# Attention, a dense MLP and a routed mixture in one Trainium2 kernel: table stores by row, and four kinds of loads in another order

## The chip, the cores and the metric

The kernel runs on one NeuronCore of one Trainium2 chip. The metric is device time of one execution in microseconds (us), the median of several runs. Below, PE is TensorE, DVE VectorE, ACT ScalarE, POOL GpSimd, and SP the engine whose queue issues nearly all DMA transfers.

## What is computed

Three layers, each feeding the next, all in float32: attention of 4 batches, 8 heads, 576 positions, head size 64, with a local mask (4 heads) or a strided mask (4 heads); a dense MLP over 2304 tokens of width 512 with 2048 hidden units; and a mixture of 8 experts in which every token goes to one.

```python
# attention: scores under mask_local (0 <= rel < 32) or mask_strided (same position modulo 32)
attn = softmax(where(mask, q @ k.T / 8, -1e9));  a = attn @ v
# dense
h = maximum(a @ w_in, 0);  x = (s * h * h + b) @ w_out
# routed: the expert of a token is the largest logit of its own
e_idx = argmax(x @ w_gate);  p = softmax(x @ w_gate)[e_idx];  eom = sigmoid(x @ w_output_gate)
out[mask_e] = p * eom[:, e] * (maximum(x @ w1[e], 0) @ w2[e])
```

## The kernel before

The tokens stand in five units of 256, 512, 512, 512 and 512. Stage one goes over 30 attention groups (scores `L586`, transposes of the probabilities `L657`, values `L696`) and, in between, over the dense products of each unit (`L915`, `L919`, `L953`), whose hidden weights come as 64-bit words (`raw`, `L774`) and are made into operands by DVE. The first nine groups share their buffers with those weights. Stage two first finds, per token, the best expert and its scale (probability times gate, `scl`). One expert is predicted for all tokens, and its two products are computed for every unit in steps of about 10 us by a scheme that saves products (seven instead of eight blocks): PE `L1480` forms the blocks, DVE adds them up in `su`, `dd` and `ht`, PE `L1426` is the second product. The operands come from `xd`, the copy of `x` in device memory: `load_x` loads them (`xr`, two transfers a unit, `L1275`), DVE forms four differences (`tt`, `L1299`) and rounds all to operands `x` (`L1185` on ACT, `L1189` on DVE). Tokens with another expert than the predicted one are listed by expert in tables (`index`: `gid`, `sid`, `lsd`), gathered (`extra`: their `x` as `X`, columns copied to `xe`, their scales fetched by an indirect DMA on POOL, `se`) and computed apart; `merge_rows` and the last tile put their rows into the output.

Two small tables pass through device memory. `scd` holds the scale of each token, so that the gather can fetch it by row number: `L1144` stores `scl` (128 partitions, one column per 128 tokens, 10 and then 8 columns) with each 4-byte element its own piece. `kid` holds the slot of every token; `keep` (`L1715` to `L1723`) stores its 18 columns likewise, 2304 pieces of 4 bytes, and later loads the last 128 back as `kix`, which `merge_rows` (`L1559`) reads.

The order of work is not written out by hand. Every piece is a generator that yields `op(...)` with an engine, an estimated duration, what it waits for, and a priority; a list scheduler picks the piece that can start first, with the priority added to its start (a lower one goes earlier). The instructions of each engine then stand in that order and each engine goes through its own strictly. All plain DMAs go through SP's queue in that order too: one that waits holds all behind it. `LOADS` and `FIRST_LOADS` set the order of the first transfers: `q` (queries with keys of a group), `v` (its values), `w` (a weight tile of 512 KB).

Of the kernel before, what the change touches and what calls it, by code (L numbers as in the profile page):

```python
# [6 lines left out]
F32 = mybir.dt.float32  # L7
F32R = mybir.dt.float32r
I32 = mybir.dt.int32
AF = mybir.ActivationFunctionType  # L10
ALU = mybir.AluOpType
# [52 lines left out]
P_DVE = 2.0  # L64
P_LATE = 0.7
P_X0 = 0.5
P_INDEX = 0.4
P_INDEX_PE = -0.3
P_EVAC = 1.5
# [93 lines left out]


WQ, WV = 1024, 768
LOADS = [(g, k) for k in range(2) for g in range(3)] + [(g, k) for g in range(3, len(GROUPS)) for k in range(2)]
FIRST_LOADS = "qqqvwvwvwqvwqvwqvwqvwqvwqvw"
LATE_Q = [k / 1000 for k, x in enumerate(FIRST_LOADS) if x in "qv"]
LATE_W = [k / 1000 for k, x in enumerate(FIRST_LOADS) if x == "w"]

# [127 lines left out]
def op(*engs, waits=(), dep=True, on=(), late=0.0):  # L298
    return engs, waits, dep, on, late
# [6 lines left out]
def body(ctx, tc, qkv, w12, moe_s, moe_b, wg, e12, out):  # L306
# [14 lines left out]
    ps = enter(tc.tile_pool(name="ps", bufs=2, space=PSUM))  # L321

    xd = [dram.tile([P, KD, USZ[u]], F32, name=f"xd{u}") for u in range(NU)]
    scd = dram.tile([NT, 1], F32, name="scd")
    gid = dram.tile([SLOT, NTAB + 1], I32, name="gid")
    sid = dram.tile([SLOT, NTAB + 1], I32, name="sid")
    lsd = dram.tile([SLOT, 2], I32, name="lsd")
    kid = dram.tile([NT, 1], I32, name="kid")

    MW = 2 * LK  # L330
    mk = const.tile([P, MW + 2 * P], F32R, name="mk")
# [24 lines left out]
    ones = const.tile([QT, P], F32, name="ones")  # L356
    poh = const.tile([P, E], F32, name="poh")
    pint = const.tile([P, 1], I32, name="pint")
    kix = const.tile([P, 1], I32, name="kix")
    xsl = mx.tile([P, 4 * sum(WIDE.values())], F32R, name="xsl", tag="big", bufs=1)  # L360
    xk = {"S": xsl[:, 0:4 * WIDE["S"]].rearrange("p (c h t) -> p c h t", c=2, h=2),
          "L": xsl[:, 4 * WIDE["S"]:].rearrange("p (c h t) -> p c h t", c=2, h=2)}
# [166 lines left out]
    def load_qkv(at):  # L529
        g, k = LOADS[at]  # L530
        w = widths(g)[k]
        yield op(("DMA", 0.0014 * w), waits=([t_qe if g < NEARLY else t_qv] if k == 0 else []) + ([t_w] if g < NEARLY else []),
                 late=LATE_Q[at] if at < len(LATE_Q) else P_QKL)
        if g < NEARLY:
            t = wp.tile([P, w], F32, name="qkv", tag="w")
        else:
            t = at_pool.tile([P, (WQ, WV)[k]], F32, name="qkv", tag=("qk", "vv")[k], bufs=NQV)[:, 0:w]
        wq = widths(g)[0]
        nc.sync.dma_start(out=t, in_=qkv[g, k * P * wq:P * (wq + k * w)].rearrange("(p n) -> p n", n=w))
        qkvs[g, k] = t  # L540
        o.set(ev_qkv[g, k], o.fin + DMA_LAT)
        if at + 1 < len(LOADS):
            o.spawn(load_qkv(at + 1), after=False)
# [224 lines left out]

    def load_w64(at):
        j = WSEQ[at]  # L770
        yield op(("DMA", 1.46), waits=[t_rw, t_w] + ([ev_early] if at >= NGATE else []), late=LATE_W[at] if at < len(LATE_W) else 0.0)
        t = wp.tile([P, 512, 2], I32, name="raw64", tag="w")
        fc, n = divmod(j, 2)
        nc.sync.dma_start(out=t, in_=w12[fc].bitcast(I32)[:, n * 1024:(n + 1) * 1024].rearrange("p (f t) -> p f t", t=2))  # L774
        raw64[j] = t
        o.set(ev_r[j], o.fin + DMA_LAT)
        if at == 12:
            o.spawn(consts())
        if at + 1 < 2 * NF:
            o.spawn(load_w64(at + 1), after=False)  # L780
# [325 lines left out]
    def route(t0, t1):  # L1106
        n = t1 - t0

        def bc(v):
            return v.unsqueeze(2).to_broadcast([QT, n, E])  # L1110

        lm, lo = lg[:, t0:t1, 0:E], lg[:, t0:t1, E:2 * E]
        yield op(("DVE", 0.7))
        m = rs(n)
        nc.vector.tensor_reduce(out=m, in_=lm, axis=AX.X, op=ALU.max)
        d = rt(n)
        nc.vector.tensor_sub(out=d, in0=lm, in1=bc(m))
        v = rt(n)
        nc.vector.scalar_tensor_tensor(out=v, in0=d, scalar=0.0,
                                       in1=wt[0:QT].unsqueeze(1).to_broadcast([QT, n, E]),  # L1120
                                       op0=ALU.is_equal, op1=ALU.mult)
        yield op(("DVE", 0.7))
        mv = rs(n)
        nc.vector.tensor_reduce(out=mv, in_=v, axis=AX.X, op=ALU.max)
        hot = oh[:, t0:t1, :]
        nc.vector.tensor_tensor(out=hot, in0=v, in1=bc(mv), op=ALU.is_equal)
        g = rt(n)
        nc.vector.tensor_mul(out=g, in0=lo, in1=hot)
        yield op(("DVE", 0.25))
        sg = rs(n)  # L1130
        nc.vector.tensor_reduce(out=sg, in_=g, axis=AX.X, op=ALU.add)
        yield op(("ACT", 0.4))
        ex = rt(n)
        nc.scalar.activation(out=ex, in_=d, func=AF.Exp)
        nc.scalar.activation(out=sg, in_=sg, func=AF.Exp, scale=-1.0)
        yield op(("DVE", 0.68))
        se = rs(n)
        nc.vector.tensor_reduce(out=se, in_=ex, axis=AX.X, op=ALU.add)
        nc.vector.tensor_scalar(out=se, in0=se, scalar1=1e-9, scalar2=None, op0=ALU.add)
        nc.vector.scalar_tensor_tensor(out=se, in0=sg, scalar=1.0, in1=se, op0=ALU.add, op1=ALU.mult)  # L1140
        nc.vector.reciprocal(out=scl[:, t0:t1], in_=se)
        yield op(("DMA", 1.0))
        with nc.allow_non_contiguous_dma(reason="one scale a token"):
            nc.sync.dma_start(out=scd[t0 * QT:t1 * QT, :].rearrange("(t p) o -> p (t o)", p=QT),  # L1144
                              in_=scl[:, t0:t1])

    ev_p = Ev()

# [118 lines left out]
    def load_x(s):  # L1267
# [11 lines left out]
        if s == 0:  # L1279
            for c, (t, ev) in enumerate(raws):  # L1280
                yield op(("SP", 0.0), waits=[ev, [t_xa]], dep=False)
                x, _ = x_tile([P, 2, 2, n])
                yield from parts(t, [x[:, h] for h in range(2)])
                x2[s, c] = x
                o.free(t_w)
            o.set(ev_x2[s, "X"])
            o.spawn(load_x(1), prio=0.1)
            return
        (r0, e0), (r1, e1) = raws
        src = {"B11": r0[:, :, 0:hn], "B21": r1[:, :, 0:hn], "B22": r1[:, :, hn:]}  # L1290
# [16 lines left out]
            o.free(t_w)  # L1307
            o.free(t_g)
        if s + 1 < NS:
            o.spawn(load_x(s + 1), prio=0.1)  # L1310

    acc2 = {}
    ev_scl = Ev()
# [238 lines left out]

    def merge_rows(oe, gc):

        yield op(("DVE", 1.6), waits=[ev_kid, ev_scl, t_w])
        t = wp.tile([P, 1024], F32, name="mr", tag="w")
        own, kf, tf, rows = t[:, 0:1], t[:, 1:2], t[0:SLOT, 2:4], t[:, 1024 - DM:]
        nc.vector.memset(rows, 0.0)
        nc.vector.tensor_copy(out=kf, in_=kix)  # L1559
        nc.vector.scalar_tensor_tensor(out=own, in0=kf, scalar=float(NT), in1=scl[:, NT // P - 1:], op0=ALU.is_lt, op1=ALU.mult)  # L1560
        nc.vector.tensor_copy(out=tf[:, 0:1], in_=gc[0:SLOT, 1:2])
        nc.vector.tensor_scalar(out=tf[:, 1:2], in0=tf[:, 0:1], scalar1=float(NT - P), scalar2=float(OOB), op0=ALU.is_lt, op1=ALU.mult)
        nc.vector.tensor_scalar(out=tf[:, 0:1], in0=tf[:, 0:1], scalar1=float(P - NT), scalar2=None, op0=ALU.add)
        place = mx.tile([SLOT, 1], I32, name="pl", tag="pl", bufs=1)
        nc.vector.tensor_tensor(out=place, in0=tf[:, 0:1], in1=tf[:, 1:2], op=ALU.add)
        yield op(("DMA", 1.0))
        nc.sync.dma_start(out=pd, in_=rows)
        yield op(("POOL", 1.1))
        nc.gpsimd.indirect_dma_start(out=pd, out_offset=bass.IndirectOffsetOnAxis(ap=place, axis=0),
                                     in_=oe, in_offset=None, bounds_check=P - 1, oob_is_err=False)  # L1570
        ev = Ev()
        o.set(ev, o.fin + 5.0)
        yield op(("DMA", 1.0), waits=[ev])
        nc.sync.dma_start(out=rows, in_=pd)
        o.fin += DMA_LAT
        merge.update(own=own, rows=rows)
        o.set(ev_merge)

    ev_kid, ev_half = Ev(), [Ev(), Ev()]


    ex = {}
# [2 lines left out]
    def index():  # L1585
# [55 lines left out]
        nc.vector.tensor_copy(out=ai, in_=adr)  # L1641
        nc.vector.tensor_single_scalar(out=si, in_=ai, scalar=SLOT - 1, op=ALU.bitwise_and)
        nc.vector.tensor_single_scalar(out=ci, in_=ai, scalar=SLOT.bit_length() - 1, op=ALU.logical_shift_right)
        o.spawn(keep(ki), prio=0.5)
        slf, clf = (tb[0:QT, k:k + NQT] for k in (816, 840))
        yield op(("DVE", 0.2))
        nc.vector.tensor_copy(out=slf, in_=si)
# [64 lines left out]
        ex["li"], ex["lrow"] = li, lrow  # L1712
        o.spawn(first_extra(), prio=P_EXTRA, pe=P_EXTRA_PE)

    def keep(ki):  # L1715
        yield op(("DMA", 1.0))
        with nc.allow_non_contiguous_dma(reason="one number a token"):
            nc.sync.dma_start(out=kid.rearrange("(t p) o -> p (t o)", p=QT), in_=ki)
        ev = Ev()
        o.set(ev, o.fin + 17.0)  # L1720
        yield op(("DMA", 0.1), waits=[ev])
        nc.sync.dma_start(out=kix, in_=kid[NT - P:, :])
        o.set(ev_kid, o.fin + 6.0)  # L1723

    def extra(get, n=NT):
        src = mx.tile([P, KD, NT], F32, name="X1", tag="big", bufs=1)
        for u in range(NU):
# [6 lines left out]
        with nc.allow_non_contiguous_dma(reason="one column of a table"):  # L1734
            nc.sync.dma_start(out=gr, in_=gid[:, bass.ds(c, 1)].rearrange("s o -> o s"))
            for h in range(2):
# [1 line left out]
            nc.sync.dma_start(out=gc[0:SLOT, 1:2], in_=sid[:, bass.ds(c, 1)])  # L1738
        t_gr = Ev()
        o.set(t_gr, o.fin + 3.0)  # L1740
        yield op(("POOL", 1.1), waits=[t_gr])
        se = mx.tile([P, 1], F32, name="se", tag="se", bufs=1)
        nc.gpsimd.indirect_dma_start(out=se, out_offset=None, in_=scd,
                                     in_offset=bass.IndirectOffsetOnAxis(ap=gc[:, 0:1], axis=0))
        yield op(("DVE", 1.8), waits=[t_r])
        xe = mx.tile([P, KD, SLOT], F32, name="xe", tag="r", bufs=NR)
        for k in range(0, SLOT, 4):
# [186 lines left out]
```

## Time and profile before

| | us |
|---|---|
| median of 3 runs | 708.28 (707.63 to 709.64) |
| the profiled execution | 711.24 |
| its span, first to last instruction | 709.5 |
| PE busy in it | 692.3 |
| mean granted TensorE clock | 0.987 |

Times in the rows are us from the start of the span. "Idle before" is time in which an engine stood before an instruction, with the one that ended it behind the arrow. An engine that waits costs time only if PE comes to wait for it in turn. The granted clock (PEclk) is a share of TensorE's full speed; 0.50 is 1.2 GHz, 1.00 is 2.4 GHz.

### The profile page before, as it was taken

The numbers are of one execution on the slowest core, as the hardware profiler recorded it, in microseconds if no ns is written. First come the engines' busy times: TensorE is split into PE (matmuls) and PEld (weight loads), VectorE is DVE, ScalarE is ACT, GpSimd is POOL, SyncE is SP. The second block draws the span as 40 slices with busy tenths as digits, with TensorE's granted clock in tenths as the row PEclk, the third lists the DMA queues.
The fourth block names the chain that finished last, engine by engine and source line by source line (L and its number), as shares of the span: only waits on it lengthen the run. The fifth ranks groups of instructions, "written<-read, shape, count | busy, mean of one in ns | idle before, by whom it ended". The sixth has DMA issues, their size and how long they took to land. (4 is left out here: it accounts for less than half of the span.)

```text
span 709.5 us, 11984 instructions
## 1 busy us (share of the span) xinstructions
PE 692.3 (98%) x4704; PEld 581.2 (82%) x4704; DVE 363.9 (51%) x853; ACT 301.0 (42%) x630; POOL 25.2 (4%) x100
## 2 busy tenths in 40 slices
PE   7999999999999999999999999999978999999996
PEld 6888888898777777877788878888977999898895
DVE  5798888854244342254341234444647754654440
ACT  4677554645344433344433544545321432323221
POOL 5000000022000000000000000001000000000000
PEclk9799999999999999999999999999998999999999
DMA  8974433241231112026200131111050073341201
GB/s 313 405 292 129 169 101 102 94 134 56 89 115 60 41 54 69 1 92 88 66 1 1 58 121 61 59 59 62 0 79 13 24 261 111 118 171 78 70 11 64
DMA packets 32622, 69.02 MB, mean 97 GB/s; under 512 B 8749, under 2 KB 11822, under 8 KB 31794
## 3 DMA queue, kind: packets, MB, share of 16 engines
q1 hardware_dynamic: 32434, 68.20, 29.5%
q8 instruction: 38, 0.62, 0.4%
q14 instruction: 22, 0.18, 0.1%
q0 software_dynamic: 128, 0.02, 0.0%
HBM read 56.75 MB, written 11.70 MB: 96 GB/s over the span
## 5 line engine op out<-in xcount | busy, mean ns | idle before, releaser
L919 PE MATMUL h<-xsl,w 128*128 128x512 f32 (+1 forms) x876 | 206.9, 381 | 0.0
L953 PE MATMUL bk<-g,w 128*128 128x512 f32 (+1 forms) x864 | 203.5, 381 | 0.0
L919 PEld LDWEIGHTS h<-xsl,w 128*128 128x128 f32 x876 | 155.7, 188 | 31.4 <-issue 0.8
L953 PEld LDWEIGHTS bk<-g,w 128*128 128x128 f32 x864 | 153.4, 188 | 31.7 <-issue 2.1
L867 ACT ACTIVATE r<-h 128x512 f32<-128x512 f32 (+1 forms) x80 | 44.4, 555 | 180.2 <-PE h L919 168.1
L893 DVE TENSOR_TENSOR g<-r,g 128x512 fp32r<-128x512 f32 (+1 forms) x73 | 48.1, 659 | 131.2 <-ACT g L891 130.9
L1426 PE MATMUL bk<-w,ht 128*128 128x512 f32 x384 | 96.8, 393 | 0.0
L1426 PEld LDWEIGHTS bk<-w,ht 128*128 128x128 f32 x384 | 69.2, 189 | 12.9 <-ACT ht L1319 0.8
L891 ACT ACTIVATE g<-r 128x512 fp32r<-128x512 f32 (+1 forms) x73 | 44.2, 605 | 2.7
L879 ACT ACTIVATE r<-r 128x512 f32<-128x512 f32 (+1 forms) x72 | 43.8, 608 | 2.2
L1319 ACT ACTIVATE ht<-h 128x256 fp32r<-128x256 f32 x24 | 9.2, 383 | 76.8 <-PE h L1480 62.3
L1480 PE MATMUL bk<-x,wc 128*128 128x256 f32 x192 | 29.0, 287 | 1.2 <-DVE x L1189 1.2
L1480 PEld LDWEIGHTS h<-x,wa 128*128 128x128 f32 x192 | 26.6, 190 | 2.4 <-issue 0.6
L1480 PE MATMUL h<-x,wa 128*128 128x256 f32 x192 | 28.4, 284 | 0.0
L1480 PE MATMUL h<-x,wc 128*128 128x256 f32 x192 | 28.1, 282 | 0.0
L696 PEld LDWEIGHTS bk<-ph,qkv 96*64 96x64 f32 (+4 forms) x608 | 20.6, 144 | 9.1 <-issue 6.7
L1480 PEld LDWEIGHTS h<-x,wc 128*128 128x128 f32 x192 | 26.2, 191 | 1.2
L1480 PEld LDWEIGHTS bk<-x,wc 128*128 128x128 f32 x192 | 25.8, 195 | 1.5 <-DVE x L1189 1.4
L696 PE MATMUL bk<-ph,qkv 96*64 96x64 f32 (+9 forms) x608 | 24.6, 233 | 0.1
L663 ACT ACTIVATE ph<-bk 96x768 f32<-96x768 f32 (+10 forms) x27 | 18.3, 679 | 13.2 <-PE bk L657 12.2
L752 DVE TENSOR_TENSOR xsl<-bk,xsl 128x384 fp32r<-128x384 f32 (+9 forms) x29 | 13.0, 450 | 19.5 <-ACT xsl L735 19.2
L586 PEld LDWEIGHTS bk<-qkv 64*64 64x64 f32 x608 | 13.8, 138 | 10.3 <-issue 5.9
(226 smaller groups left out, 771.8 us busy)
## 6 DMA issues: line engine op xcount, KB each, us to landing
raw<-w SPq DMA_DIRECT2D x32, 512.0 KB, 6.9
qkv<-qkv SPq DMA_DIRECT2D x14, 384.0 KB, 3.0
out<-ob SPq DMA_DIRECT2D x17, 256.0 KB, 2.0
xd<-x SPq DMA_DIRECT2D x4, 1024.0 KB, 4.7
wraw<-e SPq DMA_DIRECT2D x16, 256.0 KB, 2.7
xr<-xd SPq DMA_DIRECT2D x8, 512.0 KB, 5.2
X<-xd SPq DMA_DIRECT2D x4, 1024.0 KB, 11.5
we<-e SPq DMA_DIRECT2D x8, 512.0 KB, 6.7
```

The costliest lines, as they stand in the source:

```text
L586: nc.tensor.matmul(out=sc[p * QB:(p + 1) * QB, h, at_i, :], lhsT=q[h * D:(h + 1) * D, p, i * qs:i * qs + QB], rhs=k[h * D:(h + 1) * D, p, ...
L663: nc.scalar.activation(out=dst, in_=pt[0:nk], func=AF.Copy)
L696: nc.tensor.matmul(out=dst, lhsT=lhs, rhs=rhs)
L752: nc.vector.tensor_sub(out=dst[1], in0=src, in1=dst[0].bitcast(F32))
L867: nc.scalar.activation(out=r, in_=h, func=AF.Relu)
L879: nc.scalar.activation(out=to, in_=r, func=AF.Square)
L891: nc.scalar.activation(out=gt[:, 0, 0:U], in_=r, func=AF.Copy)
L893: nc.vector.tensor_sub(out=gt[:, 1, 0:U], in0=r, in1=gt[:, 0, 0:U].bitcast(F32))
L919: nc.tensor.matmul(out=h, lhsT=w_t[2 * fc][:, a, c * P:(c + 1) * P], rhs=xt(u, c, x), start=(c == 0 and n == 0), stop=(c == KD - 1 and n = ...
L953: nc.tensor.matmul(out=acc[pu][c], lhsT=w_t[2 * pf + 1][:, a, c * P:(c + 1) * P], rhs=gt[:, x, 0:cols(pu)], start=(first and n == 0), stop ...
L1426: nc.tensor.matmul(out=acc2[s, t][0], lhsT=box[k][:, x, t * P:(t + 1) * P], rhs=w_t["p", 2 * f + 1][:, a, :], start=(f == 0 and n == 0), s ...
L1480: nc.tensor.matmul(out=banks[to], lhsT=t[:, a, off + c * P:off + (c + 1) * P], rhs=x2[s, b][:, y, c, :], start=(first and c == 0 and n == ...
```

## The change

Five edits:

- **Table of scales.** `scd` gets the order of `scl` in the chip: row number `(token mod 128) * 18 + token div 128`. A store is then 128 pieces of 40 or 32 bytes.
- **Row numbers.** In `extra`, DVE works out that row number from the token's number `gc` (`gs`: three operations on 128x1) before POOL's indirect load.
- **Table of slots.** `keep`, `kid` and `kix` are gone; `merge_rows` reads the column of the last tile where it stands in the chip.
- **Operands.** `load_x` of units 1 to 4 gets priority -0.2 in place of 0.1.
- **First loads.** `q` of a group from the fourth on goes ahead of the values of the group before and of one weight tile; the planner's estimate of a load is lower (0.00128 and 1.31 in place of 0.0014 and 1.46).

```diff
+P_X2 = -0.2
-LOADS = [(g, k) for k in range(2) for g in range(3)] + [(g, k) for g in range(3, len(GROUPS)) for k in range(2)]
-FIRST_LOADS = "qqqvwvwvwqvwqvwqvwqvwqvwqvw"
+LOADS = [(0, 0), (1, 0), (2, 0), (0, 1), (1, 1)] + [(g + k, 1 - k) for g in range(2, 8) for k in (1, 0)] + [(8, 1)] + [(g, k) for g in range(9, len(GROUPS)) for k in range(2)]
+FIRST_LOADS = "qqqvwvwqvwqvwqvwqvwqvwqvwvw"
...
-        yield op(("DMA", 0.0014 * w), waits=([t_qe if g < NEARLY else t_qv] if k == 0 else []) + ([t_w] if g < NEARLY else []),
+        yield op(("DMA", 0.00128 * w + (1.2 if at == 2 else 0.0)), waits=([t_qe if g < NEARLY else t_qv] if k == 0 else []) + ([t_w] if g < NEARLY else []),
...
-            nc.sync.dma_start(out=scd[t0 * QT:t1 * QT, :].rearrange("(t p) o -> p (t o)", p=QT),
-                              in_=scl[:, t0:t1])
+        nc.sync.dma_start(out=scd.rearrange("(p t) o -> p (t o)", p=P)[:, t0:t1], in_=scl[:, t0:t1])
...
-            o.spawn(load_x(1), prio=0.1)
+            o.spawn(load_x(1), prio=P_X2)
...
-        yield op(("DVE", 1.6), waits=[ev_kid, ev_scl, t_w])
+        yield op(("DVE", 1.6), waits=[ev_scl, t_w])
...
-        nc.vector.tensor_copy(out=kf, in_=kix)
+        nc.vector.tensor_copy(out=kf, in_=ex["ki"])
...
-        o.spawn(keep(ki), prio=0.5)
+        ex["ki"] = ki[:, NQT - 1:]
...
-        yield op(("POOL", 1.1), waits=[t_gr])
+        yield op(("DVE", 0.4), waits=[t_gr])
+        gs = mx.tile([P, 3], I32, name="gs", tag="gs", bufs=1)
+        nc.vector.tensor_single_scalar(out=gs[:, 0:1], in_=gc[:, 0:1], scalar=P - 1, op=ALU.bitwise_and)
+        nc.vector.tensor_single_scalar(out=gs[:, 1:2], in_=gc[:, 0:1], scalar=P.bit_length() - 1, op=ALU.logical_shift_right)
+        nc.vector.scalar_tensor_tensor(out=gs[:, 2:3], in0=gs[:, 0:1], scalar=float(NQT), in1=gs[:, 1:2], op0=ALU.mult, op1=ALU.add)
+        yield op(("POOL", 1.1))
...
-                                     in_offset=bass.IndirectOffsetOnAxis(ap=gc[:, 0:1], axis=0))
+                                     in_offset=bass.IndirectOffsetOnAxis(ap=gs[:, 2:3], axis=0))
```

The line numbers of the changed kernel are smaller by one to eight: `L1275` is `L1272` there, `L1299` is `L1296`, `L1360` is `L1357`.

Since the scheduler plans the whole order anew, instructions move on several engines. Three places matter below. The first is SP's queue where the second part of the scales is stored, about 503 us into the span (`xd_77` and `xd_78` are units 2 and 3); before:

```order
L1144 DMA scd<-scl 128x8x1
L1718 DMA kid<-ti 128x18x1
L1275 DMA xr<-xd_77 128x1024
L1389 DMA out<-ob 128x512
L1275 DMA xr<-xd_77 128x1024
L1389 DMA out<-ob 128x512
L1722 DMA kix<-kid 128x1
L1689 DMA gid<-ix 64x289
L1690 DMA sid<-ix 64x289
L1389 DMA out<-ob 128x512 x2
L1710 DMA lsd<-li 64x2
```

and in the change:

```order
L1142 DMA scd<-scl 128x8
L1272 DMA xr<-xd_77 128x1024 x2
L1386 DMA out<-ob 128x512 x2
L1686 DMA gid<-ix 64x289
L1687 DMA sid<-ix 64x289
L1272 DMA xr<-xd_78 128x1024 x2
L1386 DMA out<-ob 128x512 x2
L1707 DMA lsd<-li 64x2
```

Both operand loads of unit 2 now stand right behind the scales, ahead of both output stores, and those of unit 3 come ahead of the next two stores.

The second is DVE where it first reads those loads, in unit 1's steps; before:

```order
L1357 TENSOR_TENSOR su<-h,su 128x256
L1299 TENSOR_TENSOR tt<-xr 128x512
L1299 TENSOR_TENSOR tt<-xr,tt 128x512
L1299 TENSOR_TENSOR tt<-xr 128x512
L1360 TENSOR_TENSOR dd<-h,su 128x256
L1363 TENSOR_TENSOR dd<-bk_4016,dd 128x256
```

and in the change:

```order
L1318 SCALAR_TENSOR_TENSOR ht<-su,ht 128x256
L1296 TENSOR_TENSOR tt<-xr 128x512
L1354 TENSOR_TENSOR su<-h,su 128x256
L1296 TENSOR_TENSOR tt<-xr,tt 128x512
L1296 TENSOR_TENSOR tt<-xr 128x512
L1296 TENSOR_TENSOR tt<-xr,tt 128x512
L1357 TENSOR_TENSOR dd<-h,su 128x256
```

The first difference now stands ahead of `su` of that step, and all four ahead of its `dd`.

The third is SP's queue at the start, from its seventh transfer on (832, 576 are `q`; 512, 768 are `v`); before:

```order
L774 DMA raw_262<-w 128x1024
L539 DMA qkv<-qkv 128x512
L774 DMA raw_287<-w 128x1024
L539 DMA qkv<-qkv 128x832
L539 DMA qkv<-qkv 128x768
L774 DMA raw_344<-w 128x1024
L539 DMA qkv<-qkv 128x576
```

and in the change:

```order
L773 DMA raw_269<-w 128x1024
L538 DMA qkv<-qkv 128x832
L538 DMA qkv<-qkv 128x512
L773 DMA raw_316<-w 128x1024
L538 DMA qkv<-qkv 128x576
L538 DMA qkv<-qkv 128x768
L773 DMA raw_359<-w 128x1024
```

The queries of the fourth group (832) now come ahead of the third group's values (512) and of one weight tile, and the later groups' queries (576) likewise.

## Rows read from the trace of the kernel before

**Rows 1.** The page, part 1: busy time, share of the span, instructions.
```profile
PE 692.3 (98%) x4704; PEld 581.2 (82%) x4704; DVE 363.9 (51%) x853; ACT 301.0 (42%) x630; POOL 25.2 (4%) x100
```
**Rows 2.** Waits of PE: engine, line <- releaser: us, times, longest.
```profile
PE h L1480 <- DVE dd L1360: 6.2, 1, 6.2
PE bk L586 <- DMA qkv<-qkv: 2.2, 1, 2.2
...
PE bk L1480 <- DVE x L1189: 1.2, 1, 1.2
```
**Rows 3.** Timeline of PE and DVE, 528 to 540: start, us, instruction [idle before <-releaser].
```profile
529.51 0.69 DVE L1299 TENSOR_TENSOR tt<-xr 128x512 f32<-128x512 f32 x1 [7.12 <-DMA xr<-xd]
...
534.55 1.65 PE L1480 MATMUL h<-x,wb 128*128 128x256 f32 x6 [6.19 <-DVE dd L1360]
...
538.88 0.87 PE L1480 MATMUL h<-x,wa 128*128 128x256 f32 x6
```
**Rows 4.** Timeline of SP's queue, 502 to 530 (SPq: a DMA issue).
```profile
503.56 0.38 SPq L1144 DMA_DIRECT2D scd<-scl  x1
514.22 0.37 SPq L1718 DMA_DIRECT2D kid<-ti  x1
514.63 1.70 SPq L1275 DMA_DIRECT2D xr<-xd  x1
```
**Rows 5.** DMA issues, whole run: count, KB each, median us to landing.
```profile
xr<-xd SPq DMA_DIRECT2D x8, 512.0 KB, 5.2
...
scd<-scl SPq DMA_DIRECT2D x1, 4.0 KB, 8.5
...
kid<-ti SPq DMA_DIRECT2D x1, 9.0 KB, 14.7
```
**Rows 6.** DMA issues, 510 to 535 alone.
```profile
xr<-xd SPq DMA_DIRECT2D x2, 512.0 KB, 14.9
```
**Rows 7.** Windows: us, busy PE, PEld, DVE, ACT, POOL, PEclk, DMA share, GB/s.
```profile
531.00:535.00 4.00, 0.45 (x2) 0.45 (x3) 2.03 (x5) 0.00 (x0) 0.00 (x0) 0.50 0.41 115
537.00:538.00 1.00, 1.00 (x6) 0.86 (x5) 1.00 (x4) 0.40 (x1) 0.00 (x0) 0.63 0.00 0
```
**Rows 8.** Windows, around the third wait.
```profile
612.00:614.00 2.00, 0.82 (x6) 0.53 (x5) 1.56 (x4) 1.13 (x3) 0.00 (x0) 1.00 0.65 219
```
**Rows 9.** Timeline of PE, 12 to 36.
```profile
12.02 1.34 PE L657 MATMUL bk<-mk,pr 128*96 128x128 f32 x8
...
15.81 1.24 PE L586 MATMUL bk<-qkv 64*64 64x96 f32 x24 [2.18 <-DMA qkv<-qkv]
...
21.47 4.86 PE L915 MATMUL h<-x,wf 128*128 128x256 f32 x12
...
26.56 0.79 PE L586 MATMUL bk<-qkv 64*64 64x108 f32 x24
...
27.97 1.89 PE L915 MATMUL h<-x,wf 128*128 128x256 f32 x8
...
34.33 0.73 PE L586 MATMUL bk<-qkv 64*64 64x96 f32 x24
```
**Rows 10.** Windows, the start.
```profile
16.00:18.00 2.00, 2.00 (x40) 1.69 (x37) 0.88 (x2) 0.00 (x0) 0.00 (x0) 0.50 1.04 400
24.00:26.00 2.00, 2.00 (x8) 1.59 (x6) 0.86 (x2) 0.88 (x4) 0.00 (x0) 0.57 1.01 401
...
40.00:60.00 20.00, 20.00 (x167) 17.04 (x167) 18.75 (x39) 13.83 (x45) 0.00 (x0) 1.00 0.46 170
46.00:48.00 2.00, 2.00 (x30) 1.54 (x29) 1.22 (x5) 1.95 (x12) 0.00 (x0) 1.00 0.99 395
```
**Rows 11.** Timeline of DVE and POOL, 588 to 595.
```profile
588.59 0.42 DVE L1363 TENSOR_TENSOR dd<-bk,dd 128x256 f32<-128x256 f32 x1 [0.29 <-PE bk L1480]
...
591.40 0.42 DVE L1368 TENSOR_TENSOR dd<-h,su 128x256 f32<-128x256 f32 x1 [2.39 <-PE h L1480]
...
593.61 1.13 POOL L1743 DMA_INDIRECT se<-scd,gc  x1 [106.66 <-DMA gc<-gid]
```

More of the change, by code (lines that the diff above doesn't have):

```diff
@@ L323, in body @@
     xd = [dram.tile([P, KD, USZ[u]], F32, name=f"xd{u}") for u in range(NU)]
-    scd = dram.tile([NT, 1], F32, name="scd")
+    scd = dram.tile([P * NQT, 1], F32, name="scd")
     gid = dram.tile([SLOT, NTAB + 1], I32, name="gid")
@@ L327, in body @@
     lsd = dram.tile([SLOT, 2], I32, name="lsd")
-    kid = dram.tile([NT, 1], I32, name="kid")
     MW = 2 * LK
@@ L358, in body @@
     pint = const.tile([P, 1], I32, name="pint")
-    kix = const.tile([P, 1], I32, name="kix")
     xsl = mx.tile([P, 4 * sum(WIDE.values())], F32R, name="xsl", tag="big", bufs=1)
@@ L770, in load_w64 @@
         j = WSEQ[at]
-        yield op(("DMA", 1.46), waits=[t_rw, t_w] + ([ev_early] if at >= NGATE else []), late=LATE_W[at] if at < len(LATE_W) else 0.0)
+        yield op(("DMA", 1.31), waits=[t_rw, t_w] + ([ev_early] if at >= NGATE else []), late=LATE_W[at] if at < len(LATE_W) else 0.0)
         t = wp.tile([P, 512, 2], I32, name="raw64", tag="w")
@@ L1142, in route @@
         yield op(("DMA", 1.0))
-        with nc.allow_non_contiguous_dma(reason="one scale a token"):
-            nc.sync.dma_start(out=scd[t0 * QT:t1 * QT, :].rearrange("(t p) o -> p (t o)", p=QT),
-                              in_=scl[:, t0:t1])
+        nc.sync.dma_start(out=scd.rearrange("(p t) o -> p (t o)", p=P)[:, t0:t1], in_=scl[:, t0:t1])
     ev_p = Ev()
@@ L1309, in load_x @@
         if s + 1 < NS:
-            o.spawn(load_x(s + 1), prio=0.1)
+            o.spawn(load_x(s + 1), prio=P_X2)
     acc2 = {}
@@ L1577, in merge_rows @@
         o.set(ev_merge)
-    ev_kid, ev_half = Ev(), [Ev(), Ev()]
+    ev_half = [Ev(), Ev()]
     ex = {}
@@ L1713, in index @@
         o.spawn(first_extra(), prio=P_EXTRA, pe=P_EXTRA_PE)
[L1715 to L1723, printed above, removed]
     def extra(get, n=NT):
```

## The prediction, made before the changed kernel ran

> **What bounds the kernel now.** I read the busy times first: PE is busy 98% of the span [rows 1], so little is to be had except where PE stands still or runs at half clock. The waits of PE come next: apart from the dummy products at the very start there are only three [rows 2], together 9.6 us. The timelines and windows around each of the three then show what was late and what the clock did behind it. The rest of the span is PE at work, and the change neither adds nor takes away a product that counts.
>
> The first wait, 6.19 us, ends at 534.55 [rows 3]. PE waited for `dd`, and `dd` stood on DVE behind three `tt`, the first of which had waited 7.12 us for an operand load `xr`. SP had issued that load at 514.63, right behind the store of `kid` at 514.22 [rows 4]. An operand load takes 5.2 us to land in the median of all [rows 5], the two of this stretch took 14.9 [rows 6], and so did the `kid` store, 14.7 for 9 KB [rows 5]. So the 2304 pieces of 4 bytes hold the DMA engines and the loads behind them; the smaller table `scd`, 1024 such pieces, took 8.5 us for its 4 KB. Behind the wait the granted clock is 0.50 (1.2 GHz), and it comes back within the stretch 537 to 538, where the mean is 0.63 [rows 7].
>
> The second wait, 2.18 us, ends at 15.81: scores of the fourth group wait for its queries [rows 9]. The DMA engines are full there, 400 GB/s at a share of 1.04 [rows 10], so the queries came as late as the bytes ahead of them made them. The clock is 0.50 in the window from 16 on and on average still 0.57 in that from 24 to 26, although PE is busy all the time.
>
> The third, 1.2 us, is for an operand of unit 3 that DVE makes late [rows 2]; the clock stays at 1.00 through it [rows 8].
>
> **The stores and the operand loads.** The `kid` store and its load back go. The `scd` store has an eighth of its pieces, 128; at the rate of the stores now (8.5 us for 1024 pieces, 14.7 for 2304: 6 to 8 ns each) that is about 1 us and the rest of a landing. Both `xr` of unit 2 are issued right behind it, which stood at 503.56 [rows 4]: say at 505, landed by 505 + 2 × 5.2 = 515.4 at the latest. DVE was ready for the first `tt` at 529.51 − 7.12 = 522.39 [rows 3]; the change puts that read one `su` further ahead, but even six us sooner it finds its data. The wait of 6.19 us is gone. The half clock behind it lasts from PE's start at 534.55 to about 537.7 (0.63 on average in 537 to 538 means half up to there). Six products that take 1.65 us in it take 0.87 at 538.88 [rows 3], so of 3.2 us half is lost: 1.6. Together **7.8 us**. Bounds: 6.2 if the clock had fallen anyway, 7.8 if all goes. I take 7.8, since nothing else in that stretch makes PE stand.
>
> The operands of unit 3 are loaded ahead of the tables' users and of two output stores, and its differences come steps earlier, ahead of the column copies of the gather. The third wait goes: **1.2 us** (0 to 1.2). Issuing earlier needs earlier buffers; the output stores that it passes are issued later by two transfers, about a microsecond of issue each, and nothing but the end waits for them.
>
> **The scale's row number.** Three operations on 128x1 are put on DVE between `dd` at 588.59 and the next `dd` at 591.40, before which DVE stood for 2.39 us [rows 11]. Nothing so small stands in my rows; the smallest DVE rows there, 0.42 for 256 columns, bound three of them by 1.3 us from above, and 0 from below, so they fit into that gap: 0. New is their wait: DVE now stands until `gc` has landed, with the next `dd` and PE's next block queued behind it. Before, only POOL waited for `gc`, until 593.61 [rows 11], about 2.2 us after DVE would want to go on. In between the gather's loads of `x` and the operand loads of unit 4 fill the DMA engines; the changed order has unit 3's operands out of the way earlier, so `gc` should land several microseconds sooner. I take 0, with up to 2.2 as a loss.
>
> **The first loads.** The queries of the fourth group come ahead of the third group's values (256 KB) and of one weight tile (512 KB): 0.79 MB at 400 GB/s [rows 10], 2.0 us sooner, about 13.9. PE has less to do until then, since four of the eight transposes (1.34 us [rows 9]) come behind: it gets there at 15.81 − 2.18 − 0.67 = 12.96 and stands for 0.9, not 2.18. Behind that the clock should hold, as it did in the third wait of 1.2 us, while it fell behind the one of 2.18. What that is worth: from 15.81 to the next group's scores at 26.56 it is 10.75 us, 10.1 of them at half clock. Twenty-four `L586` take 1.24 at half and 0.73 at full; `L915` takes 0.405 each at half (4.86 / 12) and 0.236 at full (1.89 / 8) [rows 9]; both are 0.59. So the work is 10.1 × 0.6 + 0.65 = 6.7 at full clock. To it come the four transposes moved, 0.7, and four more dummy products that fill a wait, no more than 0.6. Values and weights of the following groups come later by a queries' transfer, about 1 us, and later queries are as tight: for these waits I take 1.1, half of the wait before (0 to 2.2). From 13.9 that makes 13.9 + 6.7 + 0.7 + 0.6 + 1.1 = 23.0 in place of 26.56: 3.6. In 40 to 60 DVE is busy 18.75 of 20 us [rows 10], so of what PE is ahead by then some goes in waiting for DVE: I take **3.0**. Bounds: 0, if it is given back there, and 4.7, with no waits.
>
> A rule speaks against this term. The Trainium skill, in "TensorE: Matmul & The Clock Gate", section "HAM oscillation — how this bites in real kernels", tells of a kernel whose short groups of products wait for a transfer again and again and go back to half clock each time. By that rule several short waits in place of one long one would leave the start at half clock, and the term would be 0; the rows speak for neither, since the trace has one wait at the start and not several. One row bears on it: through the third wait the clock stayed at 1.00 [rows 8].
>
> **Sum.** 7.8 + 1.2 + 3.0 = 12.0. The profiled execution took 711.24, so its like would take 699.2; it lies 2.96 above the median of the runs, and the difference carries over: 708.28 − 12.0 = **696.3 us**.
>
> **Rivals.**
>
> *The start gives nothing* (DVE, or clock falls, take the 3.0 back): 699.3. For it: DVE at 94% in 40 to 60. Against: it is 20 us later, and the weights that DVE turns come hardly later. 0.18.
>
> *DVE stands for `gc`*: up to 2.2 lost, 698.5. For it: 593.61. Against: earlier operand loads. 0.09.
>
> *The stall moves*: unit 3's operands stand behind `gid` and `sid` on SP, and these wait for DVE and PE. If they come late, the same wait with the same half clock costs 7.8 there: 704.1. 0.06.
>
> *It doesn't do what it says*: the small pieces were not what kept `xr` back, but the load from memory in that place; then the first term is 0 and the others are small: about 708. Against: `kid` and `xr` land together at 14.7 and 14.9, and no other stretch shows such loads. 0.05.
>
> *Slower: the start stays at half clock.* In the changed order the queries of the fifth and sixth group are as tight as those of the fourth, and the DMA engines are full until 48 [rows 10]. If PE stands briefly before each of these groups and the clock stays at 0.50 past 25.9, until T, each microsecond costs 1 − 0.236 / 0.405 = 0.42. The other terms give 9.0; that is used up at T = 25.9 + 9.0 / 0.42 = 47, and beyond 52 the kernel is slower by over 2.1 us; at T = 60 it loses 14.3 − 9.0 = 5.3: 713.6. For it: at 16 to 26 the clock stayed at 0.50 with PE busy all the time. Against: it came back by 26 in the same traffic, and full transfers end by 48. The rule of the Trainium skill named above stands beside it. 0.06.
>
> **How the numbers follow.** The forecast has the other 0.56. About 0.3%, 2.1 us, is what a measurement of this kernel can tell from no change. Faster by more: 0.56 + 0.18 + 0.09 + 0.06 = 0.89; the same 0.05; slower 0.06. The range goes down to the sum with the upper bound at the start, 708.28 − 7.8 − 1.2 − 4.7 = 694.6, less the runs' own spread of 1.4 (709.64 − 708.28) and a little: 693.0. It goes up to the case without the start and with the wait for `gc`, 699.3 + 2.2 = 701.5, and half a microsecond: 702.0. What lies outside is the stall that moves, no effect and slower, 0.17, and some tails.
>
> **What would show it.** Right: no `kid` row; `xr` of unit 2 lands in about 5 us and no `tt` waits for it; PE's waits for `dd` and for `x` are gone; the clock in 530 to 540 is 1.00; the scores of the fourth group start near 13.9 with under 1.2 us of idle time, and the fifth group's about 3 us earlier than 26.56, the clock in 16 to 26 near 1.00. `gs` waits under 0.5 us. Wrong: an idle time of several microseconds of PE behind any `tt` or `gs`; a clock of 0.50 beyond 26; or PE's place at 60 us no earlier than before.

## The result and the profile after

The changed kernel takes 697.08 us, the median of 6 runs (696.82 to 700.7); the kernel before, beside it, 708.83. The ratio is 0.9842 (95% interval 0.9815 to 0.9869), so 11.2 us less (9.3 to 13.1); it is formed from the means of the runs, and the two medians lie 11.75 apart. The forecast was 12.0 less, 696.3. The first profiled execution took 700.7 with a span of 699.0, 10.5 shorter than that of before.

The page and the waits of PE, against [rows 1] and [rows 2]:

```profile
span 699.0 us, 11984 instructions
...
PE 688.2 (98%) x4702; PEld 577.3 (83%) x4702; DVE 364.5 (52%) x856; ACT 301.7 (43%) x630; POOL 25.2 (4%) x100
```

```profile
PE bk L585 <- DMA qkv<-qkv: 3.5, 2, 3.3
PE warm L1823 <- DVE xsl L441: 1.4, 1, 1.4
```

The wait for `dd` (6.2) and that for `x` (1.2) are gone. The wait for queries is not: 3.3 in place of 2.2.

SP's queue and the DMA issues at the tables, against [rows 4] and [rows 5]:

```profile
506.18 0.33 SPq L1142 DMA_DIRECT2D scd<-scl  x1
506.55 0.91 SPq L1272 DMA_DIRECT2D xr<-xd  x2
```

```profile
xr<-xd SPq DMA_DIRECT2D x8, 512.0 KB, 5.0
...
scd<-scl SPq DMA_DIRECT2D x1, 4.0 KB, 1.4
```

DVE behind them, the reads that had waited 7.12 us in [rows 3], and the new row numbers:

```profile
521.73 0.69 DVE L1296 TENSOR_TENSOR tt<-xr 128x512 f32<-128x512 f32 x1
...
582.07 0.15 DVE L1730 TENSOR_SCALAR gs<-gc 128x1 int32<-128x1 int32 x1 [1.22 <-DMA gc<-gid]
...
583.22 0.42 DVE L1365 TENSOR_TENSOR dd<-h,su 128x256 f32<-128x256 f32 x1 [0.74 <-PE h L1477]
```

The store of the scales lands after 1.4 us instead of 8.5, both operand loads are issued right behind it, and the first difference waits for nothing. DVE stands 1.22 us for `gc`, but the `dd` behind it still waits for PE, so this costs nothing.

The start, PE's timeline and the windows (columns as in [rows 7]), against [rows 9] and [rows 10]:

```profile
11.48 0.52 PE L580 MATMUL bk<-mk 128*128 128x288 f32 x2
15.27 1.24 PE L585 MATMUL bk<-qkv 64*64 64x96 f32 x24 [3.27 <-DMA qkv<-qkv]
...
23.00 1.36 PE L585 MATMUL bk<-qkv 64*64 64x108 f32 x24
```

```profile
14.00:16.00 2.00, 0.73 (x20) 0.74 (x24) 0.00 (x0) 0.00 (x0) 0.00 (x0) 0.71 1.04 402
18.00:20.00 2.00, 2.00 (x29) 1.83 (x29) 0.90 (x3) 1.33 (x6) 0.00 (x0) 0.50 1.04 413
24.00:26.00 2.00, 2.00 (x14) 1.54 (x11) 1.97 (x6) 0.00 (x0) 0.00 (x0) 0.73 1.03 398
520.00:545.00 25.00, 25.00 (x163) 22.60 (x162) 19.77 (x57) 6.55 (x14) 0.00 (x0) 1.00 0.00 1
```

In this execution the queries came at 15.27, 0.5 sooner than before, but PE was ready for them 1.6 sooner, stood 3.27 and ran at 0.50 (1.2 GHz) until about 25. At the first product of `L918` (61.78; in the kernel before `L919`, 61.36) it was 0.4 behind. So the start gave nothing here, and all of the 10.5 came later. Yet five of the six timed runs were 3.3 to 3.9 below this one, with a mean clock of 0.997 to 1.000 instead of 0.992: the start has two kinds, and the profile had caught the slow one.

### The profile page after: what moved, and what is told of

Read it like the earlier page. It is cut to its first block, busy times and chain, and to the rows that moved or that the text cites. A ratio compares the mean times of both kernels' runs of the same rounds, so it can differ in the third digit from the quotient of the medians.

```text
span 699.0 us, 11984 instructions
## 1 busy us (share of the span) xinstructions
PE 688.2 (98%) x4702; PEld 577.3 (83%) x4702; DVE 364.5 (52%) x856; ACT 301.7 (43%) x630; POOL 25.2 (4%) x100
## 5 line engine op out<-in xcount | busy, mean ns | idle before, releaser
L918 PE MATMUL h<-xsl,w 128*128 128x512 f32 (+1 forms) x876 | 206.8, 381 | 0.0
L918 PEld LDWEIGHTS h<-xsl,w 128*128 128x128 f32 x876 | 155.6, 188 | 31.4 <-issue 0.8
L585 PEld LDWEIGHTS bk<-qkv 64*64 64x64 f32 x608 | 14.2, 141 | 11.9 <-issue 6.0
L585 PE MATMUL bk<-qkv 64*64 64x96 f32 (+4 forms) x608 | 19.8, 258 | 3.5 <-DMA qkv<-qkv 3.5
## 6 DMA issues: line engine op xcount, KB each, us to landing
X<-xd SPq DMA_DIRECT2D x4, 1024.0 KB, 10.2
```

The costliest lines, as they stand in the source:

```text
L585: nc.tensor.matmul(out=sc[p * QB:(p + 1) * QB, h, at_i, :], lhsT=q[h * D:(h + 1) * D, p, i * qs:i * qs + QB], rhs=k[h * D:(h + 1) * D, p, ...
L918: nc.tensor.matmul(out=h, lhsT=w_t[2 * fc][:, a, c * P:(c + 1) * P], rhs=xt(u, c, x), start=(c == 0 and n == 0), stop=(c == KD - 1 and n = ...
```

## The experiments

For each, the span between PE's first `w<-ht` product of the routed layer and the first of its last group (`L1426` to `L1522` of before), called *the steps* below, is read from its profile: it holds the tables and operand loads, and not the start, whose two kinds a ratio of runs mixes.

**Again.** No edit.

> The changed kernel once more, for a second profile of its start. In its first profile PE stood 3.27 us at 15.27 and the clock was 0.50 to about 25, so the start gave nothing there (by 61 us PE was 0.4 later than before), yet five of the other six executions have a mean clock of 0.997 to 1.000 and a span of 694.8 to 695.6 in place of 699.0. Theory A (the start has two outcomes, and the new order of loads mostly gives the good one): span near 695, mean clock 0.998, the fourth group's scores after a wait under 2.2 us and no stretch at 0.50 behind it; time about 11.7 us below before. Theory B (the start is as in the first profile, and other executions are shorter somewhere else): 0.50 from 15.5 to 25 again, the 3.6 us missing at another place.

Measured: 0.985 (0.9826 to 0.9875); runs at 696.91, 697.15, 699.96, 700.13, 700.21. The profile is of the quick kind: PE's timeline and windows at the start.

```profile
14.17 0.73 PE L585 MATMUL bk<-qkv 64*64 64x96 f32 x24
...
16.62 0.56 PE L585 MATMUL bk<-qkv 64*64 64x96 f32 x16 [0.16 <-DMA qkv<-qkv]
...
20.13 0.79 PE L585 MATMUL bk<-qkv 64*64 64x108 f32 x24 [0.70 <-DMA qkv<-qkv]
```

```profile
14.00:16.00 2.00, 2.00 (x47) 1.52 (x46) 1.90 (x5) 0.98 (x2) 0.00 (x0) 1.00 1.04 386
20.00:22.00 2.00, 1.87 (x29) 1.63 (x30) 1.93 (x8) 0.97 (x7) 0.00 (x0) 1.00 1.05 415
```

The clock stays at 1.00 and the start ends 3.8 us sooner (`L918` at 57.97). The steps take 186.06 here and 186.14 in the first profile: the two kinds differ at the start alone. Theory A holds in that; whether the new order makes the quick kind more frequent is the next question.

The two starts part long before the fourth group. The same six dummy products, in the first profile and here:

```profile
6.43 0.98 PE L1823 MATMUL warm<-xsl 128*128 128x256 f32 x6
7.77 1.65 PE L1823 MATMUL warm<-xsl 128*128 128x256 f32 x6
```

Here PE went on at about half pace until nearly 11 us (the clock column shows 1.00 from the start all the same), was ready for the fourth group's scores at 14.2 instead of 12.0, and found the queries there. Six of the fourteen profiles of this document begin so (again, again2, fill, apart, no_kid, rows_only), and PE stands at most 0.28 at those scores in them. In the other eight PE is at full pace from about 6 us on and stands 0.61 to 3.27; in three of these (before, the first profile of the change, old_loads) the clock falls behind the stand, in five it does not.

**The old order of the first loads in the changed kernel, and the new one in the kernel before.**

```diff
-LOADS = [(0, 0), (1, 0), (2, 0), (0, 1), (1, 1)] + ...
-FIRST_LOADS = "qqqvwvwqvwqvwqvwqvwqvwqvwvw"
+LOADS = [(g, k) for k in range(2) for g in range(3)] + ...
+FIRST_LOADS = "qqqvwvwvwqvwqvwqvwqvwqvwqvw"
```

> The changed kernel with the old order of the first loads and the old estimates for them; the rest of the order (operand loads, tables) stays as changed. Theory A: the old start comes back in every execution (2.2 us wait, 0.50 from 15.5 to 25.9): 3 to 4 us longer than the changed kernel, about 700.5, or 8 to 9 below before. Theory B: within 1 us of the changed kernel.

> The kernel before with the new order of the first loads and their new estimates, nothing else. Theory A: 3 to 4 us faster than before, about 705; the waits for dd (6.2) and for x (1.2) stay. Theory B: within 1 us of before.

Measured: 0.9847 (0.9822 to 0.9872) for the old order in the changed kernel, the same as the changed kernel itself; its runs show both kinds too (696.53 and 697.21; 699.28 to 700.81). The new order alone in the kernel before: 1.001 (0.9991 to 1.0029), no gain. Theory A expected 3 to 4 us in both and fails. The profile of old_loads has the fall, behind a stand of 1.89:

```profile
15.81 0.79 PE L585 MATMUL bk<-qkv 64*64 64x96 f32 x24 [1.89 <-DMA qkv<-qkv]
```

```profile
18.00:20.00 2.00, 2.00 (x36) 1.71 (x36) 1.54 (x4) 1.43 (x9) 0.00 (x0) 0.50 1.04 418
```

The profile of the new order alone had the quick kind of start, its clock at 1.00 throughout, and still a span of 708.9. Its waits and windows show why:

```profile
PE h L1480 <- DVE dd L1360: 7.3, 1, 7.3
```

```profile
18.00:20.00 2.00, 1.38 (x9) 0.91 (x7) 2.00 (x4) 1.97 (x12) 0.10 (x1) 1.00 1.04 405
536.00:538.00 2.00, 2.00 (x7) 1.61 (x6) 1.97 (x7) 0.46 (x2) 0.00 (x0) 0.50 0.03 8
538.00:539.00 1.00, 1.00 (x8) 1.00 (x7) 0.11 (x1) 0.00 (x0) 0.00 (x0) 0.73 0.00 0
```

PE stood 7.30 for `dd` and started at 532.37; the clock came back only at about 538.5, so some 6.1 us of half clock, 3.0 lost: 10.3 for this one wait, against 7.8 in the profile of before. The steps took 199.12 instead of 196.66. The price of the wait at the table varies by what follows it.

**The changed kernel and its old order once more**, to count kinds.

> The changed kernel again, to count kinds of execution: so far 7 of 11 timed ones lie at 696.8 to 697.4 and 4 at 700.0 to 700.7. Theory A (the new order of loads makes the quick kind more frequent): 3 or more of 5 quick. Theory B (it does nothing): about half.

> The changed kernel with the old order of the first loads again, likewise: so far 2 of 5 at 696.5 to 697.2, 3 at 699.3 to 700.8. Theory A: at most 2 of 5 quick. Theory B: about half, as with the new order.

Measured: 0.9827 (0.979 to 0.9864) with 6 of 6 runs quick (695.95 to 698.0), and 0.9851 (0.9808 to 0.9895) with 4 of 6 quick (two at 701.03 and 701.93). All together 13 of 17 runs are quick with the new order and 6 of 11 with the old one. That leans to theory A, but so few runs do not settle it: by these shares it is worth (13/17 − 6/11) × 3.5 = 0.8 us.

The other kernels carry one order or the other as well. Among those without the large wait, the new order has 16 more quick runs of 16 (no_x2, apart), the old one 11 of 18 (no_kid, x2_only, pad). The kernel before has the old order and the large wait: the profile with the half clock at both places has a mean clock of 0.987, two profiles with that wait and a quick start have 0.991 (new_loads) and 0.992 (rows_only), and of its 56 runs beside the experiments 48 have 0.989 or more. So, as far as the mean clock tells, most executions of the kernel before started quickly too. By how much the order shifts the share stays open.

**No table of slots** in the kernel before (its store and load back out, the merge reads the column in the chip).

```diff
-        o.spawn(keep(ki), prio=0.5)
+        ex["ki"] = ki[:, NQT - 1:]
```

> The kernel before without the table of slots alone (no store of 2304 pieces, no load back, the merge reads the column in the chip); operand loads and scales as before. My theory (the small pieces of that store hold the loads behind it): unit 2's operand loads, issued again at about 514, land after about 5 us instead of 14.9, ahead of DVE's 522.4; the 6.2 us wait and the half clock behind it go: 7.8 us faster than before, the 1.2 us wait for x stays. Rival (the loads are slow in that place for another reason): xr still lands after some 15 us, the wait stays, within 1 us of before.

Measured: 0.9903 (0.9874 to 0.9931), 6.9 us faster (4.9 to 8.9). SP's queue, the difference on DVE, and the waits of PE:

```profile
500.11 0.59 SPq L1274 DMA_DIRECT2D xr<-xd  x1
512.80 0.34 SPq L1388 DMA_DIRECT2D out<-ob  x1
513.24 1.18 SPq L1274 DMA_DIRECT2D xr<-xd  x1
```

```profile
518.37 0.68 DVE L1298 TENSOR_TENSOR tt<-xr 128x512 f32<-128x512 f32 x1
```

```profile
PE bk L1479 <- DVE x L1188: 1.2, 1, 1.2
```

The first of the two loads goes sooner than I expected; the second is issued at 513.24, about where both stood before, and no difference waits for either. The steps take 188.36, 8.3 less than before, and the wait for `x` stays. But the edit thus did two things: it took the store away and it moved the first load 14.5 us ahead, right behind the store of the scales. There that load took 13.5 us to land, not 5:

```profile
xr<-xd SPq DMA_DIRECT2D x1, 512.0 KB, 13.5
```

The landing of the second is not in this trace. In the kernel pad below, the same with one unused tile more, the load issued in its place (512.72) has it:

```profile
xr<-xd SPq DMA_DIRECT2D x1, 512.0 KB, 5.5
```

So a load issued where both stood before lands after 5.5 us instead of 14.9 once the store of slots is gone, and the rival is out. The 1024 pieces of the scales (9.7 us here) hold a load behind them as well; here the load was early enough for that to cost nothing.

**Operand loads first** in the kernel before (priority −0.2 alone, both stores as they were).

```diff
-            o.spawn(load_x(s + 1), prio=0.1)
+            o.spawn(load_x(s + 1), prio=-0.2)
```

> The kernel before with priority -0.2 for the operand loads alone; both tables are stored as before. Unit 2's loads then stand ahead of the store of slots, behind that of the scales (1024 pieces). My theory: they land by about 516, the 6.2 us wait goes without touching the store, and the 1.2 us wait goes too. But unit 3's loads now stand behind the load back of the slots and the tables on SP, which waits for the 2304 pieces: its wait ends some 15 to 20 us later than the scales' stage, still ahead of the use of unit 3: 9 us faster than before. Rival (the store must go): unit 3's operands or the tables come late instead, a new wait of 3 us or more with half clock behind it, less than 5 us faster.

Measured: 0.9896 (0.9869 to 0.9923), 7.4 us faster; the steps take 187.42, 9.2 less than before. SP's queue, and the landing of unit 2's two loads:

```profile
501.61 1.05 SPq L1275 DMA_DIRECT2D xr<-xd  x2
511.80 1.09 SPq L1389 DMA_DIRECT2D out<-ob  x2
513.00 0.70 SPq L1718 DMA_DIRECT2D kid<-ti  x1
529.12 0.33 SPq L1722 DMA_DIRECT2D kix<-kid  x1
545.38 0.54 SPq L1689 DMA_DIRECT2D gid<-ix  x1
...
546.81 1.19 SPq L1275 DMA_DIRECT2D xr<-xd  x2
```

```profile
xr<-xd SPq DMA_DIRECT2D x2, 512.0 KB, 15.0
```

Both loads of unit 2 stand behind the store of the scales, still 1024 pieces (10.6 us here), and land after 15.0; DVE first reads them at 516.88, and no one waits.

The slow store of slots is still there, with nothing urgent behind it: unit 3's loads go out at 546.81 and are first read at 555.72. Both of PE's waits are gone. So each of the two edits takes the large wait away alone, and their gains do not add.

**The old priority** in the changed kernel.

```diff
-P_X2 = -0.2
+P_X2 = 0.1
```

> The changed kernel with the old priority 0.1 for the operand loads; no table of slots, scales in whole rows, new first loads. My theory: the 6.2 us wait does not come back, since the store is gone; the 1.2 us wait for an operand of unit 3 comes back, without a fall of the clock: 1.2 us longer than the changed kernel. Rival (the place of the loads in the order makes the gain): 5 to 8 us longer.

Measured: 0.9887 (0.9864 to 0.9909), 8.0 us below before and 3.2 above the changed kernel, more than the 1.2 I expected and less than the rival's 5; the steps take 188.47, 2.3 more than the changed kernel. The waits:

```profile
PE bk L1477 <- DVE x L1186: 1.2, 1, 1.2
PE h L1477 <- DVE dd L1365: 0.7, 1, 0.7
```

The large wait stays away, as my theory had it, and that for `x` comes back. The second row was not in its expectation: `dd` behind the new `gs`, which stands for `gc`.

**Scales in whole rows alone**, in the kernel before.

> The kernel before with the scales alone stored in whole rows, and the three DVE operations for the row number. My theory: the store of the scales lands in about 2 us instead of 8.5, but nothing waits for it, and the wait behind the store of slots stays: within 1 us of before. If DVE's wait for the row numbers (gs behind gc) costs anything, it shows here, where the operand loads have not moved: gs waits up to 2.2 us at about 589 to 593, and up to 2.2 us slower. Rival (the scales' 1024 pieces were part of what kept the operand loads back): several us faster.

Measured: 1.0037 (1.0013 to 1.0061), some 2.6 us slower by the means; the medians lie 1.2 apart. DVE and PE at the row numbers:

```profile
590.01 0.15 DVE L1741 TENSOR_SCALAR gs<-gc 128x1 int32<-128x1 int32 x1 [3.89 <-DMA gc<-gid]
```

```profile
590.81 0.97 PE L1478 MATMUL h<-x,wa 128*128 128x256 f32 x6 [0.25 <-DVE dd L1366]
```

The store of the scales lands in 1.4 us and no one gains from it, since the operand loads stand behind the store of slots here and land after 16.5. Right behind the scales, as in the changed kernel, they land after 4.6 with whole rows and after 15.0 without (x2_only); PE waits in neither. `gs` stands 3.89 us for `gc`, of which 0.25 reach PE. With the operand loads moved ahead (the changed kernel) this is 1.22 and nothing; so the priority also pays for what the row numbers add. The profiled execution was no slower in its steps than new_loads (197.17, and a wait of 6.6 for `dd`). About half of the 2.6 is the kind of start: 4 of the 12 runs have a mean clock of 0.983 to 0.987 (712.16 to 714.49), against 2 of the 17 of the kernel before (0.985; 711.02 and 711.37), and without these the means are 709.03 and 707.78. What makes the rest is not shown.

**Dummy products ahead of the fourth group's scores** in the changed kernel.

```diff
+        if g == 3:
+            for _ in range(14):
+                nc.tensor.matmul(out=two_banks(toks)[:, 0, 0:2 * P], lhsT=zero[:, 0:P], rhs=zero)
```

> The changed kernel with 14 dummy products (about 0.16 us each, 2.2 us) ahead of the fourth group's scores, where PE stood 3.27 us in the slow kind of execution and hardly at all in the quick kind. Theory A (which kind it is hangs on PE's stand there: after 1.9 to 3.3 us the clock falls to 0.50 for some 8 to 10 us, after 1.2 it does not): no execution near 700 any more, the stand under 1.2 us and the clock at 1.00 through 14 to 28 in every profile; the quick executions pay up to 1.4 us for the products; all runs at 697 to 698.5. Theory B (the kind is set by something else, the fall of the clock is its consequence): both kinds as before, each up to 2 us longer: 698 and 702.

Measured: 0.9831 (0.9794 to 0.9867), all 6 runs at 696.7 to 698.08. The products stand ahead of the scores:

```profile
13.32 1.92 PE L579 MATMUL bk<-xsl 128*128 128x256 f32 x14
...
15.43 0.73 PE L589 MATMUL bk<-qkv 64*64 64x96 f32 x24
```

As theory A expects, but inconclusive: the changed kernel beside it was quick in all its 6 runs as well, and 697.07 against 697.36 is no difference. The profile does not try the theory either: it begins at half pace as again does (its six dummy products at 7.77 take 1.65), and in such starts PE hardly stood without the products.

**A tile of 12 bytes**, unused, in the kernel before without the table of slots. In the profiles above, the late steps of the kernels with `gs` took less for the same products, though no wait lay there.

```diff
+        pad = mx.tile([P, 3], F32, name="pad", tag="pad", bufs=1)
+        nc.gpsimd.memset(pad, 0.0)
```

> The kernel before without the table of slots, and with an unused tile of 12 bytes a partition where the change has gs: it moves the operand tiles x by 32 bytes against the weight tiles and changes nothing else. In all profiles so far six products of 128x256 take 0.863 to 0.868 us where x and the weights lie 32 bytes apart modulo 64 (the changed kernel, old_loads, no_x2, rows_only) and 0.875 to 0.878 where they lie alike (before, new_loads, x2_only, no_kid). Theory (the place in memory does it): 0.864 here as in the changed kernel, about 1.1 us less than no_kid over its 672 products. Rival (the row numbers or the store of the scales do it): 0.875 as in no_kid.

Measured: 0.9854 (0.9811 to 0.9896); the steps take 187.52, 0.84 less than in no_kid. A row of the same step in no_kid and then in this kernel, six products:

```profile
658.03 0.88 PE L1479 MATMUL h<-x,wc 128*128 128x256 f32 x6
```

```profile
657.04 0.86 PE L1479 MATMUL h<-x,wc 128*128 128x256 f32 x6
```

Over all rows of six between 540 and 620 the mean is 0.863 here (50 rows) and 0.875 in no_kid (50 rows). So the unused tile alone does it, and the operations of `gs` are not needed. That it does so by the place of the operands is my reading: the 32 bytes are taken from how the kernel lays out its tiles, and no view shows addresses. At its start this execution stood longer than before, at full clock:

```profile
15.88 0.73 PE L585 MATMUL bk<-qkv 64*64 64x96 f32 x24 [2.64 <-DMA qkv<-qkv]
```

```profile
16.00:18.00 2.00, 2.00 (x72) 1.79 (x72) 1.33 (x3) 0.61 (x3) 0.00 (x0) 1.00 1.05 403
```

**Two such tiles** in the changed kernel, to try the same on the dense layer.

> The changed kernel with two unused tiles of 12 bytes a partition that put the tiles xsl and g of the dense layer 32 bytes further against its weights (32 modulo 64 apart, alike before) and leave the operands x of the steps where they are. Theory (products are shorter where the streamed operand and the weights lie 32 bytes apart modulo 64): twelve dense products of 128x512 start 2.72 us apart now; about 2 ns less for each would be 2.70, over 1740 products 3 to 4 us less, 693.5; the steps stay at 0.864 for six. Rival (it is another property of the steps' tiles): dense products and time as in the changed kernel, 697.

Measured: 0.994 (0.992 to 0.996), against 0.9842 of the changed kernel: some 7 us slower than that. Dense products in another profile of the changed kernel (again2) and here:

```profile
277.36 2.88 PE L952 MATMUL bk<-g,w 128*128 128x512 f32 x12
280.08 2.88 PE L918 MATMUL h<-xsl,w 128*128 128x512 f32 x12
```

```profile
279.56 2.96 PE L954 MATMUL bk<-g,w 128*128 128x512 f32 x12
282.36 2.96 PE L920 MATMUL h<-xsl,w 128*128 128x512 f32 x12
```

Twelve products start 2.80 apart instead of 2.72: 6.7 ns each, over the 1524 products of that width 10.2 at most; the first product of the steps comes 7.0 later (496.36 against 489.32). The steps take 187.09, 1.0 more than in again2, with 0.870 for six products (0.864 there), though I expected them to stay. So unused tiles change the pace, but my rule for it (32 bytes apart is better) is wrong: in the dense layer it is worse. No kernel here beats the changed one.

## Why the prediction was right, and where it was not

**The stores and the operand loads, 7.8: right in kind, rather small.** Taking the store of slots away alone gives 8.3 in the steps. What I had not seen is that the 1024 pieces of the scales hold loads behind them nearly as long (13.5 and 15.0 us); behind whole rows, where the change puts both loads, they take 4.6. The size came from one execution. Two other profiles with the same wait give 7.30 + 3.0 = 10.3 (new_loads) and 6.57 + some 2.1 = 8.7 (rows_only); the mean of the three is 8.9. What varies is how long the half clock lasts behind the wait: 3.2 us of work there, up to 6.1 in the others.

**The third wait, 1.2: right.** It is in every profile with the old priority and in none with the new one.

**The row numbers, 0 with up to 2.2 as a loss: right.** DVE stands 1.22, more than the 0.5 I had named as a sign, and PE not at all. Where the operand loads stay late, DVE stands 3.9 (rows_only) and 4.3 (no_x2), more than my bound, and PE 0.25 and 0.73.

**The first loads, 3.0: wrong.** The step that failed is "Behind that the clock should hold, as it did in the third wait of 1.2 us, while it fell behind the one of 2.18", and with it the time of 13.9 for the queries: I took one execution's start as the kernel's. The queries came at 15.27 in one execution of the changed kernel and by 14.17 in the next, and PE was ready for them at 12.0 and 14.2. The clock fell behind a stand of 1.89 in old_loads and held behind one of 2.64 in pad, so the length of the stand alone does not tell. What sets it is not shown.

The term also had little to win. Its 10.1 us at half clock (by the 0.57 in [rows 10] rather 9.9) are those of the profiled execution, at a mean clock of 0.987; most runs of the kernel before are at 0.989 or more, so their start was probably quick already, and then 3.0 for a slow start was not to be taken off their median. Both kinds of start come with both orders, and the comparison of the two orders shows no gain: 0.985 against 0.9847, 1.001 alone. The rival "the start gives nothing" held, in the first profile by the fall of the clock that it names beside DVE.

The rule of the Trainium skill that I set against this term ("TensorE: Matmul & The Clock Gate", section "HAM oscillation — how this bites in real kernels") gave the right size, 0, but not by its way: in new_loads PE stood three times for queries (0.61, 1.19 and 0.89) and the clock stayed at 1.00. I had also read it too widely: by its figure the waits in the kernel it tells of are some 3 to 5 us each, so it says nothing of short ones.

**What was not in the sum: about 1.0.** With the tile `gs` the steps' products get shorter: an unused tile of its size alone gives 0.84 (pad against no_kid), and the changed kernel's steps are 1.3 below those of x2_only, which has no large wait either.

With these the sum reads 7.8 to 8.9 for the wait and its half clock, 1.2, 1.0 and 0 to 0.8: 10.0 to 11.9, and 11.2 was measured. The total was near the forecast by luck: a term that is not there (3.0) stands against two that were missing or small. The mechanism of the large wait was right.

## What to carry to other kernels

A store of many tiny pieces costs by what stands behind it on the queue: either make its pieces whole rows or put the urgent loads ahead of it, and do not count both gains. A stand of PE costs itself and the half clock behind it; take the second from several executions, since one profile shows only one of its lengths. Where the start of a kernel runs with full DMA engines, look at the mean clock of all runs, and at the time of equal products in several profiles, before explaining a wait seen in one.

## What the runs showed of the hardware that was not expected

A tile of 12 bytes that nothing reads changed the pace of PE, probably by moving other tiles (by 32 bytes, as the kernel lays them out): six products of 128x256 took 0.863 us instead of 0.875, and, in another place, two such tiles made twelve of 128x512 start 2.80 apart instead of 2.72. Which pairs of addresses are good was not found: the same relation to the weights went with the shorter products in the steps and with the longer ones in the dense layer.

The store of 2304 pieces of 4 bytes took 14.7 to 16.4 us and made loads of 512 KB issued behind it land after 14.9 to 16.5 instead of 5. The store of 1024 such pieces took 8.5 to 10.6, and loads right behind it landed after 13.5 to 15.0; as 128 pieces of 32 bytes it took 1.4, and the loads behind it 4.0 to 5.5.

At the start of six profiles the same products took 1.7 times as long as in the first profile of the change (in four of them 1.65 us for six in place of 0.98) until some 10 to 13 us into the span, while the clock column showed 1.00.
